# Splitting each large tile of high and low parts into two half tiles, the low ones 128 bytes on modulo 256

## The chip, the cores and the metric

The kernel runs on one core of one Trainium2 chip. Times are device microseconds (us) of one execution. The measure is the median of the runs; the profile is one further execution, recorded by the hardware profiler.

## What is computed

A gated mix of two branches over x, which has 2 batches of 4096 tokens with 640 features. Branch a is a spectral one: a real FFT over the 4096 tokens, at each frequency a two-layer complex perceptron in 4 blocks of 160 features with ReLU between and soft shrinkage behind, and the inverse FFT. Branch b is a GEGLU network 640 to 1728 to 640.

```python
def _A_ref(x, w1, b1, w2, b2):
    Xf = rfft2(x, axes=(1, 2))          # the axis of length 1 and the 4096 tokens
    zr, zi = Xf.reshape(B, H, Wf, NB, BS).real, ....imag
    hr = einsum('bhwni,nio->bhwno', zr, w1[0]) - einsum(..., zi, w1[1]) + b1[0]
    hi = einsum(..., zi, w1[0]) + einsum(..., zr, w1[1]) + b1[1]
    hr, hi = hr * (hr > 0), hi * (hi > 0)
    # or_, oi_: the same with w2, b2; then sign(o) * max(abs(o) - 0.01, 0)
    return irfft2(or_ + 1j * oi_)
def _B_ref(x, w_gate, w_up, w_down):
    return (gelu(x @ w_gate) * (x @ w_up)) @ w_down
g = sigmoid((x * gate_w).sum(-1, keepdims=True))
return g * a + (1 - g) * b
```

## The kernel before

Every large product is made of three TensorE products of numbers with fewer bits: each operand is split into a high part (`high`, on ScalarE, line 276) and a low part (`low`, the difference, mostly on VectorE, line 279), and a product is high by high, plus high by low, plus low by high. In TensorE's terms the first operand of a matmul call is the stationary one, loaded into the array as weights (128 x 128), and the second is the moving one, streamed past it (256 or 320 columns). Every call loads its own weights.

The work goes through three stages, in an order that is written out by hand (the pool is told to keep it).

- *Gate and up products.* `quad` and `plain` handle 128 features of the inner 1728 and 512 tokens at a time, `mixed` a remainder. `quad` uses a Strassen-like scheme: sums and differences of blocks of x (`b11`, `t1` to `t5`, ...) and of the weights (`g1`, `s1` to `s4`, ...), so that seven products do the work of eight. `prod` (line 465 on) writes out the three products of each pair, `run` (line 470 on, the matmul in line 472) issues them: stationary w (made by `w_prep`), moving x (made by `x_prep`), 256 columns. Between them, at hooks, `slots` and `spread` place small steps of preparation, and the first stage of the Fourier transform, `a_step`.
- *Middle stage.* The second stage of the transform (`fwd2`), the two layers (`mlp1`: 128 features by 256 frequencies; `mlp2`: 128 frequencies by 320 features), the splitting of the results (`y_split`) and the first stage of the inverse transform (`inv1`). `mms` (matmul in line 295) issues these, through `mm3` where all three products of a pair are written out; `rest`, `zl_load` and the list `fin` load and store between them. Loads and stores go through SyncE's queue (SP) in the order of the calls: `ld` at once, `st` when `flush` is called. `wd_load` brings the prepared weights of the final stage from DRAM (`wdf`, `wdl`) into SBUF tiles `wx`, where they stay.
- *Final stage.* 32 iterations of `down`, each seven forms of a Winograd-like scheme (`b11`, `t2`, `t3`, `t1`, `b21`, `t4`, `b22`), 144 products of 320 columns in `run` with stationary `ho` (the inner activations, split by `h_op`) and moving `wx`; and `inv2`, the last stage of the inverse transform, with 12 products of 320 columns (s2s, v) for most iterations. `h_load`, `c_load` and `v_load` fetch the inputs of the next iteration.

SBUF tiles come from five tags of equal buffers, laid out one behind the other: `small` (18 of 2560 bytes per partition), `big` (18 of 5120), `tiny` (15 of 1024), a gap of 112 floats and `mid` (14 of 4096). A `big` tile holds high and low parts side by side, for instance `[P, 5, 2, P]`: five blocks of 128 numbers, each as high, then low. The tiles of x are in `mid` as high half and low half.

```python
def big(shape, dt=F32, name="big"):
    return pool.tile(shape, dt, name=name, tag="big", bufs=18)
...
for (lh, ll), (rh, rl) in pairs:
    ops += [(lh, rh), (lh, rl)] + ([(ll, rh)] if ll is not None else [])
...
for (wh, wl), (xh, xl) in zip(ws, x):
    ops += [(wh, xh), (wh, xl), (wl, xh)]
...
ops += [(hh, wh), (hh, wl)] if j == 6 and a_ in HALF else [(hh, wh), (hl, wh), (hh, wl)]
```

Of the kernel before, what the change touches and what calls it, by code (L numbers as in the profile page):

```python
# [213 lines left out]
def spectral_mix_kernel(ctx: ExitStack, tc: tile.TileContext, a):  # L214
# [30 lines left out]
    def tiny(shape, dt=F32, name="tiny"):  # L245
        return pool.tile(shape, dt, name=name, tag="tiny", bufs=15)
# [66 lines left out]
    def w_prep(t, plain=False):  # L313
# [4 lines left out]
        def gate_high():  # L318
            o["r"] = RAW.pop(t)
            o["w0"] = big([P, 5, 2, P], F32R, name="w0")  # L320
            high(o["w0"][:, :, 0], o["r"][0])

        def up_high():
            o["w1"] = big([P, 5, 2, P], F32R, name="w1")
            high(o["w1"][:, :, 0], o["r"][1])

        def up_low():
            low(o["w1"][:, :, 1], o["r"][1], o["w1"][:, :, 0])
            WG[t] = o["w0"], o["w1"]
# [18 lines left out]
        def st2():  # L348
            low(o["w0"][:, :, 1], o["r"][0], o["w0"][:, :, 0])
# [3 lines left out]
        def st3():  # L353
            g, u = o["r"]
            e = o["s"][1]
            w2 = o["w2"] = big([P, 5, 2, P], F32R, name="w2")
            high(w2[:, 0:4, 0], o["s23"])
# [3 lines left out]
        def st4():  # L361
            if not plain:
                o["w1"] = big([P, 5, 2, P], F32R, name="w1")
            w1, w2 = o["w1"], o["w2"]
            high(w1[:, 0:2, 0], o["s"][0])
            high(w2[:, 4, 0], o["s"][1][:, 0])
            low(w2[:, 0:4, 1], o["s23"], w2[:, 0:4, 0])

        def st5():
            w1, w2 = o["w1"], o["w2"]  # L370
            o["w3"] = [tiny([P, 2, P], F32R, name="w3") for k in range(2)]
            if not plain:
                high(w1[:, 2:4, 0], o["r"][1][:, 2:4])
            high(w1[:, 4, 0], o["s"][1][:, 1])
            low(w1[:, 0:2, 1], o["s"][0], w1[:, 0:2, 0])
            low(w2[:, 4, 1], o["s"][1][:, 0], w2[:, 4, 0])

        def st6():
            w1 = o["w1"]
            for k in range(2):  # L380
                high(o["w3"][k][:, 0], o["s"][2][:, k])
            if not plain:
                low(w1[:, 2:4, 1], o["r"][1][:, 2:4], w1[:, 2:4, 0])
            low(w1[:, 4, 1], o["s"][1][:, 1], w1[:, 4, 0])

        def st7():
            w0, w1, w2, w3 = (o[k] for k in ("w0", "w1", "w2", "w3"))
            for k in range(2):
                low(w3[k][:, 1], o["s"][2][:, k], w3[k][:, 0])
            mat = lambda w, i: (w[:, i, 0], w[:, i, 1])  # L390
# [3 lines left out]
                     "s4": [(w3[0][:, 0], w3[0][:, 1]), (w3[1][:, 0], w3[1][:, 1])]}  # L394
# [152 lines left out]
    def plain(key, t, hook):  # L547
# [3 lines left out]
        for q, x0, x1 in ((0, "b11", "b21"), (1, "b12", "b22")):  # L551
            x = x_of(o, x0, x1, ("k4", q))
            for h, (dst, w) in enumerate(((pg, w0), (pu, w1))):
                k = 4 * q + 2 * h
                hook(k)
                run(dst[:, 256 * q:256 * q + 256], prod([(w[:, i, 0], w[:, i, 1]) for i in range(5)], x))
# [7 lines left out]
    def mixed(key):  # L564

        o, w = XO[key], WG[NPAIR]
        ws = [(w[:, k, 0], w[:, k, 1]) for k in range(5)]
# [13 lines left out]
    def f1_load(q):  # L581
        m = min(5, 17 - 5 * q)
        F1[q] = big([P, 5, 2, P], F32R, name="f1")
        nc.gpsimd.dma_start(F1[q][:, :m], a["f1"][:, 5 * q:5 * q + m])
# [23 lines left out]
    def a_step(b, n2, h):  # L608
        xs = XS.pop((b, n2, h))
        m = n2 if n2 < 16 else 32 - n2  # L610
        f = F1[m // 5][:, m % 5]
# [4 lines left out]
        for q in range(2):  # L616
            cs = slice(320 * q, 320 * q + 320)
            pa = bank()
            nc.tensor.matmul(pa[:, :320], f[:, h], xs[:, cs], start=True, stop=True)  # L619
# [16 lines left out]
    OUT1 = {"k": 256, 0: 0, 1: 512}  # L636
    LAST1 = (896, 768)

    def prep(l, pb):
# [13 lines left out]
        def wide_high(q):  # L653
            m = o["m"][q]
            if l == 1:
                w = dm[ns[q]] = big([P, 1024], F32R, name="wm")
                high(w[:, :P], m[:, :P], -1.0)
                high(w[:, 768:800], m[:, P:BS], -1.0)
                high(w[:, 800:832], m[:, BS:BS + 32])
                high(w[:, 896:960], m[:, BS:BS + 64])  # L660
                high(w[:, 256:768].rearrange("p (c h k) -> p c h k", c=2, h=2)[:, :, 0],
                     m[:, 224:].rearrange("p (c k) -> p c k", c=2))
                return
            w = dm[ns[q]] = big([P, 2, 480], F32R, name="wm")
            high(w[:, 0, BS:], m[:, BS:])
            high(w[:, 0, :BS], m[:, :BS], -1.0)

        def wide_low(q):
            w, m = dm[ns[q]], o["m"][q]
# [3 lines left out]
            if l == 1:  # L673
                minus(w[:, P:256], m[:, :P], w[:, :P])
                minus(w[:, 832:864], m[:, P:BS], w[:, 768:800])
                low(w[:, 864:896], m[:, BS:BS + 32], w[:, 800:832])
                low(w[:, 960:], m[:, BS:BS + 64], w[:, 896:960])
                x = w[:, 256:768].rearrange("p (c h k) -> p c h k", c=2, h=2)
                low(x[:, :, 1], m[:, 224:].rearrange("p (c k) -> p c k", c=2), x[:, :, 0])
                return  # L680
            low(w[:, 1, BS:], m[:, BS:], w[:, 0, BS:], nc.gpsimd)
            minus(w[:, 1, :BS], m[:, :BS], w[:, 0, :BS])
# [794 lines left out]
```

## Time and profile before

| | |
|---|---|
| Runs, median of 3 | 2547.68 us (2546.67 to 2549.09) |
| Span of the profiled execution | 2546.4 us |
| TensorE matmuls (PE) | 2535.1 us busy, 20276 instructions |
| TensorE weight loads (PEld) | 2530.4 us busy, 20276 instructions |
| VectorE (DVE) | 2055.1 us busy, 4212 instructions |
| ScalarE (ACT) | 1502.8 us busy, 3490 instructions |
| GpSimd (POOL) | 370.2 us busy, 370 instructions |
| DMA | 483.48 MB, 190 GB/s in the mean |

The span is the time from the first to the last instruction that the profiler recorded; here it lies just below the fastest of the timed runs. Times of TensorE come from pipelined matmuls whose ends are modelled: the duration of one matmul (276 to 309 ns) is longer than the distance from its start to the next one's, so the pace is read from the time that a known number of products takes. In the rows, `bank<-wx,ho` names the output and the inputs of an instruction; `L472` is the line that issued it; "x11736" is a count; in the engine's rows of a stretch the order is PE, PEld, DVE, ACT, POOL, then the granted clock of TensorE as a share, the DMA share and GB/s. In the chain in order of time each row has the start, the length, the engine, the tile, the line and the number of instructions.

### The profile page before, as it was taken

Reading aid. Unit: us, or ns where it says so; the run is one execution under the profiler, and the core shown is the slowest. Engines: PE = TensorE matmul, PEld = TensorE weight load, DVE = VectorE, ACT = ScalarE, POOL = GpSimd, SP = SyncE. Lnnn points to the kernel's source line nnn. Section 1 sums busy time; section 2 is a strip of 40 time slices with the busy share of each in tenths; the row PEclk is TensorE's granted clock in tenths of the full one; section 3 lists DMA queues with packets and bytes.
Section 4 is the critical chain, followed back from the end, with each engine's and each line's share of the span. In section 5 each row is a group of like instructions: output and inputs, shape, how many; then the busy total and the mean of one; then the engine's idle time right before and its main releaser. Section 6 shows DMA issues by size and latency. Waiting matters only on the chain.

```text
span 2546.4 us, 54296 instructions
## 1 busy us (share of the span) xinstructions
PE 2535.1 (100%) x20276; PEld 2530.4 (99%) x20276; DVE 2055.1 (81%) x4212; ACT 1502.8 (59%) x3490; POOL 370.2 (15%) x370
## 2 busy tenths in 40 slices
PE   9999999999999999999999999999999999999999
PEld 9999999999999999999999999999999999999999
DVE  7778777777777766776667788888899999999998
ACT  6555555666665655555556777778644444445443
POOL 0000000000000000000002111111133333333332
PEclk9999999999999999999999999999999999999999
DMA  6565657676767667776667455548844444344442
GB/s 232 190 215 196 212 170 234 205 236 211 219 205 249 207 213 231 224 230 214 212 222 223 129 153 150 160 137 266 291 149 138 150 156 158 120 144 156 155 136 92
DMA packets 346060, 483.48 MB, mean 190 GB/s; under 512 B 24701, under 2 KB 222717, under 8 KB 345797
## 3 DMA queue, kind: packets, MB, share of 16 engines
q1 hardware_dynamic: 331108, 438.47, 54.5%
q0 software_dynamic: 14688, 41.56, 4.5%
q8 instruction: 159, 2.61, 0.4%
q14 instruction: 105, 0.85, 0.1%
HBM read 300.29 MB, written 179.64 MB: 188 GB/s over the span
## 4 chain that ended last, share of the span: by engine, by line
PE 97%; DMA 1%; DVE 1%; issue 0%; ACT 0%; SPq 0%; DVEq 0%; ACTq 0%
PE bank L472 77%; PE bank L295 14%; PE bank L783 3%; PE bank L619 1%; DMA wx<-wdf 1%; PE bank L861 1%; PE bank L860 1%; DMA wx<-wdl 0%; PE bank L863 0%; DVE xo L279 0%; DMA wraw<-in_wgu_dram 0%; DVE xd L430 0%; DVE h L543 0%; DVE w L279 0%; DVE wl L715 0%
## 5 line engine op out<-in xcount | busy, mean ns | idle before, releaser
L472 PE MATMUL bank<-xo,w 128*128 128x256 f32 x11736 | 1362.0, 277 | 6.3 <-ACT xo L276 5.1
L472 PEld LDWEIGHTS bank<-xo,w 128*128 128x128 f32 x11736 | 1353.0, 188 | 7.5 <-ACT xo L276 5.1
L472 PE MATMUL bank<-wx,ho 128*128 128x320 f32 x4608 | 678.6, 308 | 0.1
L472 PEld LDWEIGHTS bank<-wx,ho 128*128 128x128 f32 x4608 | 674.1, 188 | 0.6 <-DMA wx<-wdf 0.3
L498 ACT ACTIVATE u<-bank 128x256 f32<-128x256 f32 x408 | 156.7, 384 | 258.0 <-PE bank L472 252.5
L279 DVE TENSOR_TENSOR ho<-hraw,ho 128x640 fp32r<-128x640 f32 (+3 forms) x384 | 276.9, 761 | 5.0 <-ACT ho L276 3.0
L276 ACT ACTIVATE ho<-hraw 128x640 fp32r<-128x640 f32 x320 | 166.3, 574 | 64.1 <-PE bank L472 46.8
L498 ACT ACTIVATE p<-bank 128x256 f32<-128x256 f32 x204 | 78.6, 385 | 149.0 <-PE bank L472 66.4
L279 DVE TENSOR_TENSOR xo<-xraw,xo 128x512 fp32r<-128x512 f32 x209 | 142.9, 684 | 25.2 <-ACT xo L276 24.7
L531 DVE TENSOR_TENSOR u<-bank,u 128x256 f32<-128x256 f32 x204 | 85.9, 421 | 90.8 <-ACT u L498 88.2
L279 DVE TENSOR_TENSOR xs<-xr,xs 64x640 fp32r<-64x640 f32 x128 | 105.0, 820 | 58.0 <-ACT xs L276 56.0
L1165 ACT ACTIVATE uu<-bank,gs 128x320 f32<-128x320 f32 x120 | 55.0, 525 | 160.0 <-PE bank L295 157.7
L295 PE MATMUL bank<-wm,h 128*128 128x320 f32 (+1 forms) x792 | 137.8, 309 | 0.0
L540 DVE TENSOR_TENSOR u<-bank,u 128x256 f32<-128x256 f32 x204 | 85.5, 419 | 62.2 <-PE bank L472 61.3
L276 ACT ACTIVATE xo<-xraw 128x512 fp32r<-128x512 f32 x209 | 131.0, 627 | 7.1 <-DMA xraw<-in_xT_dram 5.3
L621 DVE TENSOR_TENSOR as<-bank,as 64x320 f32<-64x320 f32 x256 | 113.9, 484 | 25.0 <-ACT as L620 24.0
L295 PEld LDWEIGHTS bank<-wm,h 128*128 128x128 f32 (+1 forms) x792 | 118.6, 185 | 1.2
L276 ACT ACTIVATE ho<-hs 128x640 fp32r<-128x640 f32 (+1 forms) x128 | 71.9, 576 | 77.8 <-PE bank L472 57.7
L572 POOL MEMSET h<- 64x512 f32 x16 | 8.4, 522 | 747.7 <-PE bank L619 369.4
L514 DVE TENSOR_TENSOR p<-bank,p 128x256 f32<-128x256 f32 x204 | 86.5, 424 | 36.6 <-PE bank L472 32.2
L279 DVE TENSOR_TENSOR s2s<-s,s2s 128x320 fp32r<-128x320 f32 x128 | 111.6, 929 | 0.9 <-ACT s2s L276 0.9
L620 ACT ACTIVATE as<-bank 64x320 f32<-64x320 f32 x256 | 96.8, 427 | 16.5 <-PE bank L619 14.0
(157 smaller groups left out, 3470.7 us busy)
## 6 DMA issues: line engine op xcount, KB each, us to landing
xo<-xD SPq DMA_DIRECT2D x124, 512.0 KB
xraw<-in_xT_dram SPq DMA_DIRECT2D x225, 256.0 KB
hD<-h SPq DMA_DIRECT2D x224, 256.0 KB
hraw<-hD SPq DMA_DIRECT2D x128, 320.0 KB
xD<-xo POOLq DMA_DIRECT2D x64, 512.0 KB, 4.4
sc<-scr SPq DMA_DIRECT2D x65, 320.0 KB
xr<-in_x_dram SPq DMA_DIRECT2D x64, 320.0 KB
scr<-as SPq DMA_DIRECT2D x64, 320.0 KB
```

Source lines behind the costliest of these rows:

```text
L276: nc.scalar.activation(dst, src, AF.Copy, scale=scale)
L279: eng.tensor_sub(dst, src, hi.bitcast(F32))
L295: nc.tensor.matmul(dst, l, r, start=i == 0, stop=i == len(ops) - 1)
L472: nc.tensor.matmul(dst, l, r, start=first and i == 0, stop=i == len(ops) - 1, skip_group_check=True)
L498: copy = lambda d, s_: nc.scalar.activation(d, s_, AF.Copy)
L514: nc.vector.tensor_add(p1, A, p1)
L531: nc.vector.tensor_add(u4, C, u4)
L540: nc.vector.tensor_add(u2, C, u2)
L620: nc.scalar.activation(stg[hi, cs], pa[lo, :320], AF.Copy)
L621: nc.vector.tensor_add(stg[hi, cs], pa[hi, :320], stg[hi, cs])
L783: nc.tensor.matmul(pz[:, kp * P:(kp + 1) * P], SC[b, c, kp][:, o:o + P], ft, start=True, stop=True)
L1165: nc.scalar.activation(uu[n2][:, cs], pe[:, :320], AF.Copy, scale=gs[:, b, 0, n2:n2 + 1])
```

## The change

The tag `big` goes; instead the tags `hi` and `lo` have 18 buffers of 2560 bytes each, and `pair` returns one tile of each. Five of the 15 `tiny` buffers become `tinyl`, for the low parts of small tiles. The order in SBUF is `small`, `hi`, `tiny`, a gap of 128 bytes, `lo`, `tinyl`, a gap of 320 bytes, `mid`; the total is the same. So `lo` and `tinyl` lie 128 bytes on modulo 256, and `mid` lies where it lay modulo 256. All users of `big` take a pair. With it come:

- `mm3` writes high by high, low by high, high by low, in place of high by high, high by low, low by high. `prod` and `down` keep their order.
- Low parts of the final stage's weights that lie in `mid` start 192 bytes in (`48:1008`); the tile of the form `t1` that lies in `mid` now holds its high parts, 64 bytes in (`16:976`), and `lo` holds its low parts.
- In the second layer the low part of the weights starts 192 bytes into its tile (`48:528`); in the first layer, narrow pieces and their low parts stay in one tile.
- Loads that filled one tile become two: in `f1_load`, `i1_load` (GpSimd's queue), `wd_load` and `zl_load` (SP's queue); the store in `rest` becomes two.
- In `w_prep` the four `high` and `low` calls of `w3` become two.

Cut to the core (the other steps of `w_prep`, `prep` and `mlp1` change their indices in the same way):

```diff
-    gap = []
-
-    def big(shape, dt=F32, name="big"):
-        return pool.tile(shape, dt, name=name, tag="big", bufs=18)
+    gaps = set()
+
+    def gap(tag, n):
+        if tag not in gaps:
+            gaps.add(tag)
+            nc.gpsimd.memset(pool.tile([P, n], F32, name="gap", tag=tag, bufs=1), 0.0)
+
+    def pair(shape, dt=F32, name="pair"):
+
+        h = pool.tile(shape, dt, name=name, tag="hi", bufs=18)
+        if not gaps:
+            nc.gpsimd.memset(tiny([P, 1], name="gap"), 0.0)
+        gap("gap1", 32)
+        return h, pool.tile(shape, dt, name=name, tag="lo", bufs=18)
 
     def mid(shape, dt=F32, name="mid"):
-        if not gap:
-            gap.extend([tiny([P, 1], name="gap"), pool.tile([P, 112], F32, name="gap", tag="gap", bufs=1)])
-            for t in gap:
-                nc.gpsimd.memset(t, 0.0)
+        if "gap2" not in gaps:
+            assert gaps
+            nc.gpsimd.memset(tinyl([P, 1], name="gap"), 0.0)
+            gap("gap2", 80)
         return pool.tile(shape, dt, name=name, tag="mid", bufs=14)
 
     def small(shape, dt=F32, name="small"):
         return pool.tile(shape, dt, name=name, tag="small", bufs=18)
 
     def tiny(shape, dt=F32, name="tiny"):
-        return pool.tile(shape, dt, name=name, tag="tiny", bufs=15)
+        return pool.tile(shape, dt, name=name, tag="tiny", bufs=10)
+
+    def tinyl(shape, dt=F32, name="tinyl"):
+        return pool.tile(shape, dt, name=name, tag="tinyl", bufs=5)
...
-            ops += [(lh, rh), (lh, rl)] + ([(ll, rh)] if ll is not None else [])
+            ops += [(lh, rh)] + ([(ll, rh)] if ll is not None else []) + [(lh, rl)]
...
         def gate_high():
             o["r"] = RAW.pop(t)
-            o["w0"] = big([P, 5, 2, P], F32R, name="w0")
-            high(o["w0"][:, :, 0], o["r"][0])
+            o["w0"] = pair([P, 5, P], F32R, name="w0")
+            high(o["w0"][0], o["r"][0])
...
-            o["w3"] = [tiny([P, 2, P], F32R, name="w3") for k in range(2)]
+            o["w3"] = tiny([P, 2, P], F32R, name="w3"), tinyl([P, 2, P], F32R, name="w3")
...
-            for k in range(2):
-                high(o["w3"][k][:, 0], o["s"][2][:, k])
+            high(o["w3"][0], o["s"][2])
...
-                low(w3[k][:, 1], o["s"][2][:, k], w3[k][:, 0])
-            mat = lambda w, i: (w[:, i, 0], w[:, i, 1])
+            low(w3[1], o["s"][2], w3[0])
+            mat = lambda w, i: (w[0][:, i], w[1][:, i])
...
-        F1[q] = big([P, 5, 2, P], F32R, name="f1")
-        nc.gpsimd.dma_start(F1[q][:, :m], a["f1"][:, 5 * q:5 * q + m])
+        F1[q] = pair([P, 5, P], F32R, name="f1")
+        for h in range(2):
+            nc.gpsimd.dma_start(F1[q][h][:, :m], a["f1"][:, 5 * q:5 * q + m, h])
...
-    OUT1 = {"k": 256, 0: 0, 1: 512}
-    LAST1 = (896, 768)
+    OUT1 = {"k": P, 0: 0, 1: 2 * P}
+    LAST1 = (512, 384)
...
-            w = dm[ns[q]] = big([P, 2, 480], F32R, name="wm")
-            high(w[:, 0, BS:], m[:, BS:])
-            high(w[:, 0, :BS], m[:, :BS], -1.0)
+            dm[ns[q]] = w[:, :480], wl[:, 48:528]
+            high(w[:, BS:480], m[:, BS:])
+            high(w[:, :BS], m[:, :BS], -1.0)
...
-            t = o["t"] = big([P, 2, 2, 320], F32R, name="wl")
+            th, tl = o["t"] = pair([P, 640], F32R, name="wl")
             o["b"] = small([66, 2, 320], F32R, name="bh")
             high(o["b"], o["s"])
-            high(t[:, :, 0], o["l"])
+            n = 320 if l == 2 else 256
+            o["h"], o["lo"] = (t[:, :2 * n].rearrange("p (q c) -> p q c", q=2) for t in (th, tl))
+            high(o["h"], o["l"][:, :, :n])
             for q in range(2):
-                dl[ns[q]] = t[:, q]
+                dl[ns[q]] = o["h"][:, q], o["lo"][:, q]
...
+        z = zmid(b, c, "zz")
+        fwd2(b, c, 4 * P, z)
+        F = width(b, c)
+        for h in range(2):
+            st(dr(zld[b][c], 2 * CW * h, [[4 * CW, P], [CW, 2], [1, F]]), z[h].bitcast(F32))
...
+        t = zmid(b, c, "zl1")
+        t2 = pair([66, 2, CW], F32R, name="zl2") if F == CW else zl2[chunks.index((b, c)) % 2]
+        for h in range(2):
+            if F == CW:
+                nc.gpsimd.memset(t2[h][64:66].bitcast(F32), 1.0)
+            ld(t[h].bitcast(F32), dr(d, 2 * h * P * CW, [[CW, P], [P * CW, 2], [1, F]]))
...
-                wh, wlo = w[:, 0, o:o + 320], w[:, 1, o:o + 320]
-                ops += [(h[0][:, r, fs], wh), (h[1][:, r, fs], wh), (h[0][:, r, fs], wlo)]
-            ops += [(hA[:, fs], wl[:, 0]), (hB[:, fs], wl[:66, 1])]
+                wh, wl = w[:, o:o + 320], wlo[:, o:o + 320]
+                ops += [(h[0][:, r, fs], wh), (h[1][:, r, fs], wh), (h[0][:, r, fs], wl)]
+            ops += [(hA[:, fs], rh), (hB[:, fs], rl[:66])]
...
-            t = YS[b, c, pb, j] = big([P, 2, 2, 320], F32R, name="ys")
-            split(t[:, 0], t[:, 1], y.rearrange("p r n o -> p r (n o)"),
+            t = YS[b, c, pb, j] = pair([P, 2, 320], F32R, name="ys")
+            split(*t, y.rearrange("p r n o -> p r (n o)"),
...
-    HI = {"b11": 0, "t2": 2, "b21": 4, "t3": 5, "t1": 6, "t4": 8, "b22": 9}
-    LO = {"b11": 1, "t2": 3, "t3": 7, "b21": 10, "b22": 11, "t4": 12}
+    HI = {"b11": 0, "t2": 1, "b21": 4, "t3": 5, "t4": 8, "b22": 9}
+    LO = {"b11": 2, "t2": 3, "t3": 6, "t1": 7, "b21": 10, "b22": 11, "t4": 12}
...
-                    st(dr(wdf[j], 320 * HI[n], [[13 * 320, P], [1, 320]]), w[:, 0].bitcast(F32))
-                    st(dr(wdl, 320 * j, [[7 * 320, P], [1, 320]]), w[:, 1].bitcast(F32))
+                    st(dr(wdf[j], 320 * LO[n], [[13 * 320, P], [1, 320]]), w[:, 1].bitcast(F32))
+                    st(dr(wdl, 320 * j, [[7 * 320, P], [1, 320]]), w[:, 0].bitcast(F32))
...
-            t = big([P, 4, 320], F32R, name="wx")
-            go(t.rearrange("p h d -> p (h d)"), wdf[j], 13, 4 * part, 4)
-            for k, (n, h) in enumerate((("b11", 0), ("b11", 1), ("t2", 0), ("t2", 1)) if part == 0 else
-                                       (("b21", 0), ("t3", 0), ("t1", 0), ("t3", 1))):
-                put(n, h, t[:, k])
+            ts = pair([P, 2, 320], F32R, name="wx")
+            for h in range(2):
+                go(ts[h].rearrange("p h d -> p (h d)"), wdf[j], 13, 4 * part + 2 * h, 2)
+            for k, (n, h) in enumerate((("b11", 0), ("t2", 0), ("b11", 1), ("t2", 1)) if part == 0 else
+                                       (("b21", 0), ("t3", 0), ("t3", 1), ("t1", 1))):
+                put(n, h, ts[k // 2][:, k % 2])
         elif part == 2:
             if j < 6:
                 t = small([P, 2, 320], F32R, name="wx")
                 go(t.rearrange("p h d -> p (h d)"), wdf[j], 13, 8, 2)
                 put("t4", 0, t[:, 0])
                 put("b22", 0, t[:, 1])
-            x = mid([P, 3, 320], F32R, name="wx")
-            later.append(lambda: go(x.rearrange("p h d -> p (h d)"), wdf[j], 13, 10, 3))
+            x = mid([P, 1024], F32R, name="wx")[:, 48:1008]
+            later.append(lambda: go(x, wdf[j], 13, 10, 3))
+            x = x.rearrange("p (h d) -> p h d", h=3)
             for k, n in enumerate(("b21", "b22", "t4")):
                 put(n, 1, x[:, k])
         else:
-            x = mid([P, 1024], F32R, name="wx")
+            x = mid([P, 1024], F32R, name="wx")[:, 16:976]
             n = 3 if j < 6 else 1
             go(x[:, :320 * n], wdl, 7, j, n)
             for k in range(n):
-                WM.setdefault(j + k, {}).setdefault("t1", [None, None])[1] = x[:, 320 * k:320 * k + 320]
+                WM.setdefault(j + k, {}).setdefault("t1", [None, None])[0] = x[:, 320 * k:320 * k + 320]
             if j == 6:
-                go(x[:, 336:976], wdf[6], 13, 8, 2)
-                put("t4", 0, x[:, 336:656])
-                put("b22", 0, x[:, 656:976])
+                go(x[:, 320:], wdf[6], 13, 8, 2)
+                put("t4", 0, x[:, 320:640])
+                put("b22", 0, x[:, 640:])
...
-        t = big([P, 5, 2, P], F32R, name="ho")
-        uh, ul = (tiny([P, 2, P], F32R, name="ho") for k in range(2))
+        th, tl = pair([P, 5, P], F32R, name="ho")
+        uh, ul = tiny([P, 2, P], F32R, name="ho"), tinyl([P, 2, P], F32R, name="ho")
         src, six = HR[i].pop(name) if name in ("s1", "s3", "s4", "a22") else HR[i][name]
-        split(t[:, :, 0], t[:, :, 1], src, eng)
+        split(th, tl, src, eng)
...
-        I1.append(big([P, 5, 2, P], F32R, name="i1"))
-        nc.gpsimd.dma_start(I1[0], a["i1"])
+        I1.append(pair([P, 5, P], F32R, name="i1"))
+        for h in range(2):
+            nc.gpsimd.dma_start(I1[0][h], a["i1"][:, :, h])
```

More of the change, by code (lines that the diff above doesn't have):

```diff
@@ L555, in plain @@
                 hook(k)
-                run(dst[:, 256 * q:256 * q + 256], prod([(w[:, i, 0], w[:, i, 1]) for i in range(5)], x))
+                run(dst[:, 256 * q:256 * q + 256], prod([(w[0][:, i], w[1][:, i]) for i in range(5)], x))
                 if k < 6:
@@ L566, in mixed @@
         o, w = XO[key], WG[NPAIR]
-        ws = [(w[:, k, 0], w[:, k, 1]) for k in range(5)]
+        ws = [(w[0][:, k], w[1][:, k]) for k in range(5)]
         pm = bank()
@@ L618, in a_step @@
             pa = bank()
-            nc.tensor.matmul(pa[:, :320], f[:, h], xs[:, cs], start=True, stop=True)
+            nc.tensor.matmul(pa[:, :320], f, xs[:, cs], start=True, stop=True)
             nc.scalar.activation(stg[hi, cs], pa[lo, :320], AF.Copy)
@@ L727, in spectral_mix_kernel, with zmid @@
     chunks = [(0, 1), (0, 0)] + [(b, c) for b in range(2) for c in range(NCH) if (b, c) > (0, 1)]
-    def zmid(b, c, shape, dt=F32, name="z"):
-        return (big if wide(b, c) else mid)(shape, dt, name=name)
+    def zmid(b, c, name):
+        if wide(b, c):
+            return pair([P, 2, CW], F32R, name=name)
+        t = mid([P, 2, 2, CH], F32R, name=name)
+        return t[:, 0], t[:, 1]
     def two(b, c, name):
@@ L862, in last @@
                                  skip_group_check=True)
[L863 removed]
+            nc.tensor.matmul(dst, rk, t1, start=False, stop=True, skip_group_check=True)
         h = two(b, c, "h")
@@ L1140, in h_op @@
             low(ul, six, uh, eng)
-        HO[i, name] = [(t[:, j, 0], t[:, j, 1]) for j in range(5)] + [(uh[:, j], ul[:, j]) for j in range(2)]
+        HO[i, name] = [(th[:, j], tl[:, j]) for j in range(5)] + [(uh[:, j], ul[:, j]) for j in range(2)]
     def inv2(i):
```

124 lines of the change are left out of this document (56 added, 68 removed).

## The prediction

> **What bounds the kernel now.** I read the page first: the busy table and the slices, then the chain, then the groups.
>
> ```profile
> span 2546.4 us, 54296 instructions
> PE 2535.1 (100%) x20276; PEld 2530.4 (99%) x20276; DVE 2055.1 (81%) x4212; ACT 1502.8 (59%) x3490; POOL 370.2 (15%) x370
> PEclk9999999999999999999999999999999999999999
> ...
> PE 97%; DMA 1%; DVE 1%; issue 0%; ACT 0%; SPq 0%; DVEq 0%; ACTq 0%
> PE bank L472 77%; PE bank L295 14%; PE bank L783 3%; PE bank L619 1%; DMA wx<-wdf 1%; PE bank L861 1%; PE bank L860 1%; DMA wx<-wdl 0%; PE bank L863 0%; DVE xo L279 0%; DMA wraw<-in_wgu_dram 0%; DVE xd L430 0%; DVE h L543 0%; DVE w L279 0%; DVE wl L715 0%
> ```
>
> TensorE is busy for 2535.1 of 2546.4 us, so at most 11.3 us are waits for other engines. Its clock is granted in full in every slice. The chain is TensorE for 97%, and 77% of the span is one line, the `run` helper. Every matmul has a weight load of its own (20276 of each), both rows are full, so each weight load runs beside the matmul before it. With no idle time to remove, only the pace of the matmuls can move the end. The chain in order of time gives that pace: start, length, line, count.
>
> ```profile
> 66.91 22.38 PE bank L472 x190
> 92.94 21.54 PE bank L472 x190
> ...
> 1879.54 1.76 PE bank L295 x12
> 1881.30 21.02 PE bank L472 x144
> 1904.08 21.02 PE bank L472 x144
> ```
>
> The first two rows are the same 190 gate/up products at two paces, 117.8 and 113.4 ns, with nothing waited for inside either. So a stretch can settle into a slow or a fast pace. The last rows are the final stage: 144 products of 320 columns at 146.0 ns each, and twelve of `inv2`, an iteration of 22.78 us, 32 times. The view of one line gives duration as least/median/most:
>
> ```profile
> engine op xcount: duration ns min/median/max, first and last start us, forms
> L472 PE MATMUL bank<-xo,w x11736: 276/276/583, 5.1 to 1386.3; 128*128 128x256 f32 x199
> L472 PE MATMUL bank<-wx,ho x4608: 302/309/414, 1812.1 to 2541.6; 128*128 128x320 f32 x192
> L295 PE MATMUL bank<-wm,h x792: 304/308/315, 1393.8 to 1806.0; 128*128 128x320 f32 x192, 128*2 128x320 f32 x6
> L295 PE MATMUL bank<-s2s,v x408: 303/308/312, 1806.4 to 2520.6; 128*128 128x320 f32 x136
> L295 PE MATMUL bank<-ys,i x392: 305/309/412, 1407.3 to 1812.0; 128*128 128x320 f32 x196
> L295 PE MATMUL bank<-z,wm x384: 277/280/294, 1387.7 to 1798.7; 128*128 128x256 f32 x180, 128*128 128x258 f32 x12
> ```
>
> In the gate/up stage the median is the least value, 276: half the products or more run unhindered. In the final stage the median stands 7 ns over the least, and the 320-column products of the middle stage 4 to 5 over theirs. Something holds these up by a few nanoseconds each, and only there.
>
> **The change part by part.** *Addresses.* I call an address modulo 256, counted from the start of `big`, its residue. Now `small`, `big` and `tiny` have residue 0 (buffer sizes 2560, 5120 and 1024 are multiples of 256) and `mid` 192 (the gap of 112 floats). What I compare is the moving operand of a product with the stationary operand loaded beside it, that of the next product; their difference is the distance.
>
> Gate/up stage: x in `mid`, weights in `big`, the distance is always 192, and the pace can be 113.4. Final stage: per form the products are (hh,wh), (hl,wh), (hh,wl); stationary parts all at 0, wh at 0, wl at 0 in three of seven forms and at 192 in four. So 17 of 21 products have distance 0, and the pace is 146.0. `inv1` (ys,i) is at 0 throughout. I read this as: distance 0 costs, and 192 need not.
>
> After the change hi lies at 0, lo at 128, `mid` still at 192 (128 + 320 = 448). In the final stage, product 1 moves wh (0) while hl (128) is loaded, product 2 moves wh (0) while hh (0) is loaded, product 3 moves wl (128) while hh (0) is loaded: distances 128, 0, 128. `inv1` gets the same through the new order in `mm3`. Distance 0 falls from 17 in 21 to 1 in 3.
>
> *The price of distance 0.* The page gives the mean of the final stage's product:
>
> ```profile
> L472 PE MATMUL bank<-wx,ho 128*128 128x320 f32 x4608 | 678.6, 308 | 0.1
> L472 PE MATMUL bank<-xo,w 128*128 128x256 f32 x11736 | 1362.0, 277 | 6.3 <-ACT xo L276 5.1
> ```
>
> 308 less the least, 302, is 6 ns; over 17/21 of the products that is 7.4 ns for each at distance 0. No row shows distance 128. From below it costs what the unhindered ones cost (saving up to 6 ns per product, 4608 x 6 = 28 us); from above it costs like 0 (saving nothing). I take it as free, since it is the farthest from 0 on a ring of 256: 1/3 x 7.4 = 2.5 ns remain of 6, a saving of 3.5 x 4608 = 16 us. For `inv1`, 309 - 302 = 7 falls to 2.5: 392 x 4.5 = 1.8 us. A loss from above can't be ruled out by a row either, but 309 is the slow pace already.
>
> [...]
>
> *Will DVE let it be faster?* Final iterations by engine (busy us and counts of PE, PEld, DVE, ACT, POOL):
>
> ```profile
> 1881.30:1904.08 22.78, 22.78 (x158) 22.78 (x158) 22.27 (x38) 11.01 (x24) 8.06 (x7) 1.00 0.48 155
> 1926.86:1949.64 22.78, 22.78 (x158) 22.78 (x158) 21.45 (x39) 11.13 (x24) 8.32 (x7) 1.00 0.46 150
> ```
>
> A saving of 3.5 x 144 = 0.5 us brings an iteration to 22.28, just what DVE needs in the worse row (22.27). DVE is the next bound: beyond 16 us it takes most of any further gain, at the better row (21.45) 1.33 x 32 = 43 us at the very most.
>
> *Gate/up.* Weight order is wh, wh, wl against x at 192: distances 192, 64, 192. None becomes 0. I take no change; the bound is the slow pace, below.
>
> *`mlp2`* (wm,h): stationary at 192, moving parts at 0 and 128 now, 0, 128, 64 and 192 after. Distances are 64, 192 and 128 today, and yet the median is 4 over the least. This row speaks against my reading. I take 0, bounds 792 x 4 = 3 us either way. `inv2` (s2s,v) keeps distance 192 and only changes order; `mlp1` (z,wm) 384 x 3 = 1 us either way.
>
> *Extra instructions.* `wd_load` issues two DMAs for one in 14 cases, `zl_load` and `rest` one more each for 16 chunks, `f1_load` and `i1_load` five more on Pool; merging the `w3` copies removes a few.
>
> ```profile
> L1048 SPq DMA_DIRECT2D wx<-wdf x28: 319/428/1212, 1721.8 to 1821.5; - x28
>   DMA wx<-wdf: 0.3, 1
> L584 POOL DMA_DIRECT2D f<-in_f_dram x4 | 2.2, 547 | 0.0
> ```
>
> SP's 46 extra issues at 0.43 us are 20 us, spread over the middle stage (about 1388 to 1821 us by the rows) and beside TensorE; Pool's five are 2.7 us on an engine 15% busy. Where the cover is thin is the start of the final stage: TensorE waited 0.3 us for wx there. Queued on SP behind the doubled loads are the later wx and hraw loads; five more issues ahead of them are 5 x 0.43 = 2.1 us, the bound of a wait. I take 0.
>
> *Buffers.* `tiny` goes from 15 to 10, with 5 in `tinyl`: per final iteration 20 tiles in 15 buffers become 13 in 10 and 7 in 5. Behind a later release wait SP's hraw loads and Pool's v load, and then Pool's subtractions, with Pool busy for 8 of 22.78 us. I take 0.
>
> The sum: 2546.4 - 16.1 - 1.8 = 2528.5 us by the profiled execution. The runs have a median 1.3 us over that execution, so 2530.
>
> **The rivals.** *The gate/up stage loses its fast pace (slower).* A third of its products get distance 64, which no row of 256 columns shows, and the two paces of the same 190 products show how little it takes. At the slow pace each costs 117.8 - 113.4 = 4.4 ns more: 11736 x 4.4 = 52 us, of which I estimate 46 as some stretches are slow already. With the 18 us gained, +28: 2576. It decides the sign from 18 us / 4.4 ns = 4100 products on, 35% of the stage. For it: the 64 and 192 of `mlp2` aren't free at 320 columns. Against it: the fast pace holds over hundreds of products and returns after interruptions, and no distance becomes 0. Chance 0.36.
>
> *Only the third product pays.* Then 3912 x 4.4 = 17 us eat the 18: no change, 2547.
>
> *Addresses don't matter.* The excess could come from 320 columns alone; then no pace moves and the time is 2548. The page SBUF — State Buffer (the Trainium skill, section Who interferes with whom) gives TensorE two independent read ports, one for the moving operand and one for the weights, and says that "PE and ACT never wait on anyone"; by that rule the change does nothing. The two paces and the 309 against 302 show matmuls held up while nothing that the profile names is waited for, which speaks against it here. With the last case, chance 0.10.
>
> *Late buffers or loads* in the final stage cost more than is gained: 32 iterations x 0.8 us = 26 us, 2556. DVE's margin of 0.5 to 1.3 us speaks for it, Pool's idle time against. It decides from 0.56 us per iteration. Chance 0.04.
>
> **How the numbers follow.** The forecast and what is better than it have 0.50: 2530, with a range of its own from 2508 (28 us, the whole excess, and 10 us from slow gate/up stretches that end) to 2542. Faster 0.50, the same 0.10, slower 0.40. The range of all cases goes from 2508 to 2584, the slow gate/up stage with half of the gain; about 1 in 10 is left out on each side. A change of 0.2%, 5 us, is what a measurement can tell here.
>
> **What would show it.** Right: iterations of the final stage near 22.3 us; the median of wx,ho near 305; DVE over 98% busy there; gate/up stretches of 190 still at 21.5 us with median 276. Wrong in the price: wx,ho still at 308 or more. Wrong by the first rival: the median of xo,w at 280 or more, stretches of 190 at 22 us or more. Wrong by late loads: idle time of PE above 11.3 us, ended by DMA wx or DVE ho.

## The result, and the profile after

The kernel after takes 2575.35 us (median of 4 runs, 2574.50 to 2576.83) against 2547.69 us; the ratio is 1.011, with a 95% interval of 1.0096 to 1.0125. It is slower by 1.1%, where 2530 us had been forecast. First the page of the kernel after, whose matmul line is now L483 and whose split lines are L289 (high) and L292 (low):

```profile
span 2572.7 us, 54415 instructions
PE 2554.5 (99%) x20276; PEld 2536.1 (99%) x20276; DVE 2086.1 (81%) x4203; ACT 1492.2 (58%) x3481; POOL 364.3 (14%) x378
PEclk9999999999999999999999999999999999999999
...
PE 89%; DVE 7%; issue 3%; ACT 1%; DMA 0%; POOL 0%; SPq 0%; ACTq 0%; DVEq 0%; POOLq 0%
...
L292 DVE TENSOR_TENSOR ho<-hraw,ho 128x640 fp32r<-128x640 f32 (+3 forms) x384 | 301.7, 826 | 5.0 <-ACT ho L289 3.0
```

The chain was TensorE for 97%; now VectorE has 7% of it, and "issue" 3%. The clock is granted in full as before. The view of the matmul line says in which stage the 26.3 us of span went (duration least/median/most, then first and last start):

```profile
L483 PE MATMUL bank<-xo,w x11736: 275/276/583, 5.2 to 1386.4; 128*128 128x256 f32 x199
L483 PE MATMUL bank<-wx,ho x4608: 304/309/419, 1812.9 to 2567.8; 128*128 128x320 f32 x192
```

The gate/up stage ends at 1386.4 us (before: 1386.3), and the final stage begins at 1812.9 us (1812.1). All but 0.8 us is lost in the final stage: 754.9 us from the first of its products to the last, where it was 729.5. The chain in order of time shows one iteration there (start, length, what):

```profile
2026.31 1.29 PE bank L308 x7
2027.60 9.43 PE bank L483 x63
2037.03 0.02 issue
2037.06 0.43 ACT ho L289
2037.48 5.82 DVE ho L292 x2
...
2046.12 0.16 ACT ho L289
...
2046.45 0.83 ACT s2s L289 x2
2047.28 0.41 DVE ho L292
2047.69 0.36 DVE s2s L292
2048.05 1.35 issue
2049.40 1.02 DVE s2s L292
2050.43 0.04 issue
2050.47 1.30 PE bank L308 x7
2051.77 9.43 PE bank L483 x63
```

From L308 to L308 that is 24.16 us, where an iteration of the kernel before takes 22.78. The chain leaves TensorE after 63 products, for a VectorE split of `ho` of 5.8 us (two instructions), and comes back with `inv2` (L308), which waited for the split of `s2s`. The same stretch in the timeline of GpSimd, then of VectorE, first before and then after (start, length, last column the idle time before and what ended it; VectorE's neighbours of one line are added up):

```profile
2047.06 0.57 POOL L976 DMA_DIRECT2D v<-in_v_dram  x1 [9.90 <-PE bank L472]
2047.65 2.70 POOL L1109 TENSOR_TENSOR hraw<-hraw 128x640 f32<-128x640 f32 x2
2050.31 1.63 POOL L1116 TENSOR_TENSOR hs<-hraw 128x640 f32<-128x640 f32 x1
2053.36 0.74 POOL L1116 TENSOR_TENSOR hs<-hraw 128x256 f32<-128x256 f32 x1 [1.43 <-ACT ho L276]
```

```profile
2047.35 3.14 DVE L279 TENSOR_TENSOR ho<-hraw,ho 128x640 fp32r<-128x640 f32 x3
...
2050.93 2.20 DVE L279 TENSOR_TENSOR ho<-hraw,ho 128x640 fp32r<-128x640 f32 x3
```

```profile
2037.33 0.58 POOL L994 DMA_DIRECT2D v<-in_v_dram  x1 [11.43 <-issue]
2037.93 2.27 POOL L1129 TENSOR_TENSOR hraw<-hraw 128x640 f32<-128x640 f32 x2
2040.15 2.25 POOL L1136 TENSOR_TENSOR hs<-hraw 128x640 f32<-128x640 f32 x2
```

```profile
2035.47 1.33 DVE L292 TENSOR_TENSOR ho<-hraw,ho 128x640 fp32r<-128x640 f32 x3
2037.06 0.49 DVE L1217 TENSOR_TENSOR e<-bank,e 128x320 f32<-128x320 f32 x1 [0.26 <-PE bank L483]
2037.47 6.15 DVE L292 TENSOR_TENSOR ho<-hraw,ho 128x640 fp32r<-128x640 f32 x3
```

In both kernels GpSimd's v load stands in front of its four subtractions (`h_s3`, `h_s2`). Before, it waited for a TensorE product (L472, which reads nothing of `tiny` but `ho`), so its buffer had held a part of an earlier `ho`. After, `tiny` has 10 buffers, and the one that the v load gets held the `hraw` piece that VectorE's split of `a12` has just left (2035.47 to 2036.8): GpSimd's queue waits for a VectorE semaphore until 2036.84, and in nearly every iteration this wait ends 0.04 us behind that split. So the v load comes after the split, 9.9 us into the iteration where it was 6.5 us, the four subtractions run as one block from 2037.93 to 2042.4, and the split of `a22` that began at 2037.47 goes on past their end: three instructions that take 1.33 us undisturbed take 6.15. Before, the subtractions met the splits of both `a12` and `a22`, with a pause of 1.43 us before the last of them, and these splits took 3.14 and 2.20 us. Over these two splits VectorE loses 2.7 us before and 4.8 after.

Two numbers come from the starts of the matmuls in the trace, first to last product of the final stage (4991 distances): the gaps (distances over 160 ns, less 146 each) and the pace (the mean of the rest). Before: 0.7 us of gaps, 146.03 ns. After: 20.2 us, 147.24 ns. 19.5 us of gaps and 4872 x 1.21 ns = 5.9 us of pace make the 25.4 us.

### The profile page after: what moved, and what is told of

Same layout as the page of the kernel before. It is cut to its first block, busy times and chain, and to the rows that moved or that the text cites. A ratio compares the mean times of both kernels' runs of the same rounds, so it can differ in the third digit from the quotient of the medians.

```text
span 2572.7 us, 54415 instructions
## 1 busy us (share of the span) xinstructions
PE 2554.5 (99%) x20276; PEld 2536.1 (99%) x20276; DVE 2086.1 (81%) x4203; ACT 1492.2 (58%) x3481; POOL 364.3 (14%) x378
## 4 chain that ended last, share of the span: by engine, by line
PE 89%; DVE 7%; issue 3%; ACT 1%; DMA 0%; POOL 0%; SPq 0%; ACTq 0%; DVEq 0%; POOLq 0%
PE bank L483 69%; PE bank L308 14%; DVE ho L292 4%; PE bank L803 3%; PE bank L631 1%; DVE s2s L292 1%; ACT s2s L289 1%; PE bank L878 1%; PE bank L879 1%; DVE uu L1222 1%; ACT ho L289 0%; PE bank L881 0%; DMA zl<-zl 0%; DMA xraw<-in_xT_dram 0%; DVE xo L292 0%
## 5 line engine op out<-in xcount | busy, mean ns | idle before, releaser
L483 PE MATMUL bank<-xo,w 128*128 128x256 f32 x11736 | 1361.0, 277 | 7.4 <-ACT xo L289 5.2
L483 PEld LDWEIGHTS bank<-xo,w 128*128 128x128 f32 x11736 | 1351.8, 188 | 8.9 <-ACT xo L289 5.2
L483 PE MATMUL bank<-wx,ho 128*128 128x320 f32 x4608 | 688.9, 310 | 0.1
L483 PEld LDWEIGHTS bank<-wx,ho 128*128 128x128 f32 x4608 | 679.9, 188 | 5.1 <-DVE ho L292 2.9
L292 DVE TENSOR_TENSOR ho<-hraw,ho 128x640 fp32r<-128x640 f32 (+3 forms) x384 | 301.7, 826 | 5.0 <-ACT ho L289 3.0
L289 ACT ACTIVATE ho<-hraw 128x640 fp32r<-128x640 f32 x320 | 169.4, 572 | 154.3 <-PE bank L483 59.9
L292 DVE TENSOR_TENSOR xo<-xraw,xo 128x512 fp32r<-128x512 f32 x209 | 142.8, 684 | 25.0 <-ACT xo L289 24.4
L292 DVE TENSOR_TENSOR xs<-xr,xs 64x640 fp32r<-64x640 f32 x128 | 105.0, 820 | 57.7 <-ACT xs L289 55.2
L289 ACT ACTIVATE ho<-hs 128x640 fp32r<-128x640 f32 (+1 forms) x128 | 69.5, 567 | 135.1 <-issue 112.6
L308 PE MATMUL bank<-wm,h 128*128 128x320 f32 (+1 forms) x792 | 137.3, 308 | 0.0
L289 ACT ACTIVATE xo<-xraw 128x512 fp32r<-128x512 f32 x209 | 131.1, 627 | 6.4 <-DMA xraw<-in_xT_dram 4.6
L308 PEld LDWEIGHTS bank<-wm,h 128*128 128x128 f32 (+1 forms) x792 | 118.3, 185 | 1.2
L292 DVE TENSOR_TENSOR s2s<-s,s2s 128x320 fp32r<-128x320 f32 x128 | 111.9, 931 | 0.5 <-ACT s2s L289 0.5
L468 POOL DMA_DIRECT2D xD<-xo x64 | 34.3, 536 | 479.3 <-DVE xo L292 388.6
```

What stands on the lines that cost most here:

```text
L289: nc.scalar.activation(dst, src, AF.Copy, scale=scale)
L292: eng.tensor_sub(dst, src, hi.bitcast(F32))
L308: nc.tensor.matmul(dst, l, r, start=i == 0, stop=i == len(ops) - 1)
L468: nc.gpsimd.dma_start(xD[key[1]][:, kept], XM.pop((key, name)).rearrange("p h n -> p (h n)").bitcast(F32))
L483: nc.tensor.matmul(dst, l, r, start=first and i == 0, stop=i == len(ops) - 1, skip_group_check=True)
```

## The experiments

All ratios are against the kernel before on the same chip; gaps and pace are read as above.

| kernel | median us | ratio (95% interval) | gaps us | pace ns |
|---|---|---|---|---|
| e1_tiny_split_only | 2560.06 | 1.0048 (1.0033 to 1.0063) | 13.1 | 146.13 |
| e2_low_at_0 | 2560.71 | 1.0051 (1.0034 to 1.0068) | 12.2 | 146.60 |
| e4_low_at_192 | 2612.09 | 1.0256 (1.0240 to 1.0271) | 14.1 | 146.67 |
| e5_v_behind | 2555.11 | 1.0029 (1.0018 to 1.0040) | 0.0 | 147.40 |
| e6_before_v_behind | 2547.06 | 0.9999 (0.9989 to 1.0008) | 0.0 | 146.03 |
| e7_low_at_0_v_behind | 2551.73 | 1.0012 (1.0002 to 1.0022) | 1.1 | 146.62 |
| e8_tiny_split_v_behind | 2548.31 | 0.9999 (0.9990 to 1.0008) | 0.7 | 146.03 |
| d64_ho_at_64 | 2554.34 | 1.0027 (1.0017 to 1.0037) | 0.7 | 147.04 |
| d192_ho_at_192 | 2552.75 | 1.0019 (1.0010 to 1.0029) | 1.2 | 146.93 |
| d128_ho_at_128 | 2546.91 | 0.9996 (0.9986 to 1.0005) | 0.5 | 145.76 |
| m0_x_at_0 | 2622.50 | 1.0296 (1.0278 to 1.0315) | 0.0 | 146.58 |
| m128_x_at_128 | 2607.31 | 1.0236 (1.0219 to 1.0252) | 0.0 | 146.71 |
| m64_x_at_64 | 2593.91 | 1.0180 (1.0163 to 1.0196) | 1.1 | 145.85 |

### One part of the change alone: the small buffers

```diff
     def tiny(shape, dt=F32, name="tiny"):
-        return pool.tile(shape, dt, name=name, tag="tiny", bufs=15)
+        return pool.tile(shape, dt, name=name, tag="tiny", bufs=10)
+    def tinyl(shape, dt=F32, name="tiny"):
+        return pool.tile(shape, dt, name=name, tag="tinyl", bufs=5)
...
-        uh, ul = (tiny([P, 2, P], F32R, name="ho") for k in range(2))
+        uh, ul = (t([P, 2, P], F32R, name="ho") for t in (tiny, tinyl))
```

> The kernel before, with one part of the change alone: the 15 tiny buffers become 10 and 5 (the low parts of ho, w3 and the small constants in the 5); big tiles stay whole, no address modulo 256 moves. Theory A (fewer tiny buffers: the v load in front of GpSimd's subtractions gets a buffer that VectorE's splitting of a12 has only just left, the four subtractions run late and in one piece, one VectorE split waits for all of them, TensorE waits for VectorE): PE gaps of about 20 us in the final stage, its pace unchanged at 146.0 ns a product, 2547.7 + 20 = 2568 us. Rival B (half tiles: the splits now write whole rows in place of strided ones and lose to GpSimd for that reason, or the shifted addresses do it): no gaps, 2548 us.

Measured: +12.5 us, 13.1 us of gaps, pace as before. The v load takes over the `hraw` piece of `a12` here too. So the buffers alone make most of the gaps, without any half tile or moved address, and rival B falls. The size was off: 13 us, not 20.

### The kernel after without the shift, and with another

```diff
-        gap("gap1", 32)
+        gap("gap1", 64)     # low parts at 0; 48: at 192
...
-            gap("gap2", 80)
+            gap("gap2", 48)     # 64
```

> The kernel after, gap1 256 bytes and gap2 192: the low half tiles lie at 0 modulo 256 instead of 128; all else as after. Theory A: gaps of about 20 us stay. For the pace of 147.2 ns: if the shift by 128 is what costs 1.2 ns a product, it returns to 146.0 and the time is 2575 - 6 = 2569 us; if the lost change of the moving operand from 0 to 192 is what costs, the pace is about 146.8, and the time 2573 us. Rival B' (the shift causes the stalls of VectorE too): 2548 us.

Measured: 2560.71 us, less than either case. The pace is 146.60 ns, near the second case, but the gaps shrink to 12.2 us, about those of the small buffers alone. So the shift by 128 bytes costs 0.64 ns a product (3 us) and 8 us of gaps; the other 2 us lie ahead of the final stage. In the trace about half of the iterations with the shift take some 24.2 us, most of these with a split of 5.6 us; without it they alternate between 23.0 and 23.45 us, with longest splits of 1.7 and 5.1 us. The starts in the traces tell the patterns apart. With the shift, the first instruction of the split of `a22` keeps its 0.81 us where it begins 0.50 us or more ahead of GpSimd's block, and is held to the block's end where it begins 0.48 us ahead or less. At 0 it leads by 0.49 to 0.51 us in every second iteration and is free there. That is 0.03 us earlier in the iteration, behind 63 products that take 0.64 ns less each, 0.04 us together. So the slower pace may be what tips it; no run changes that lead alone, and it stays open.

> The kernel after, gap1 192 bytes and gap2 256: the low half tiles lie at 192 modulo 256. Theory A: gaps of about 20 us stay. Pace: in the kernel before a product whose moving operand lies at 0 takes 143.4 ns when the next one's lies at 192, else 146 to 147; one in three is of this kind here, so (146.8 + 143.4 + 146.1) / 3 = 145.4 ns, 2575 - 1.8 x 4872 = 2566 us. If no address matters: 147.2 ns and 2575 us. In the gate/up stage stationary low parts at 192 meet x at 192; if that distance of 0 costs as in the final stage, a third of 11736 products lose 4.4 ns: +17 us.

Measured: 64.6 us slower, in a stage that wasn't the suspect. The gate/up stage:

```profile
L483 PE MATMUL bank<-xo,w x11736: 276/281/582, 5.1 to 1432.6; 128*128 128x256 f32 x199
L483 PE MATMUL bank<-wx,ho x4608: 303/308/417, 1859.3 to 2605.4; 128*128 128x320 f32 x192
```

The median goes from 276 to 281, and the final stage begins 47 us late. I had allowed for a third of the products, 17 us, but the whole stage runs at the slow pace, 117.8 ns in each of the chain's stretches of 190. That distance 0 is what does it isn't shown: with x at 64 (below) the same pace comes with no product at distance 0. The final stage didn't gain: 146.67 ns, not 145.4.

### The v load behind the subtractions

```diff
                     if k == 2 and n > 1:
                         c_load(n)
-                        v_load(n)
                     if k == 4:
                         h_s3(n, nc.gpsimd)
                         h_s2(n, nc.gpsimd)
+                        if n > 1:
+                            v_load(n)
```

> The kernel after, with the v load issued by GpSimd behind the subtractions h_s3 and h_s2 (at hook 4) instead of at hook 2; addresses, buffers and half tiles as after. Theory A: nothing late stands in front of the subtractions any more, the VectorE split of 5.6 us is back near 1.7 us, gaps fall from 20 us to a few, 2575 - 17 = 2558 us (the pace of 147.2 ns stays, which is 6 us). Rival B (half tiles or addresses): 2575 us.

Measured: 2555.11 us, all gaps gone. First its page, then its chain:

```profile
span 2553.3 us, 54409 instructions
PE 2541.3 (100%) x20276; PEld 2536.6 (99%) x20276; DVE 2057.8 (81%) x4203; ACT 1487.7 (58%) x3481; POOL 377.3 (15%) x378
```

```profile
1903.12 1.77 PE bank L308 x12
1904.89 21.23 PE bank L483 x144
1926.11 1.76 PE bank L308 x12
```

The chain runs through TensorE again, 144 products at 21.23 / 144 = 147.4 ns. One moved DMA issue gives back 20.2 of the 27.7 us with the layout and the number of buffers as in the kernel after (v, allocated later, may get another buffer than it did); the rest is nearly all pace.

> The kernel before, with the v load behind h_s3 and h_s2 as in the experiment on the kernel after. It has 15 tiny buffers and no PE gaps in the final stage to give back: 2548 us by theory A. If moving the load alone makes a kernel faster, whatever the buffers, it is below 2545 us and the 20 us regained after say nothing on the buffers.

Measured: no difference. Moving the load gains nothing where nothing waits for it, so what it regained in the kernel after was the wait.

> The kernel before with the tiny buffers split into 10 and 5, and the v load behind h_s3 and h_s2. If the 12.5 us of the split came by the v load's wait alone: no gaps, pace 146.0 to 146.1 ns, 2547 us. If fewer tiny buffers delay something else too: gaps of some us remain, 2550 to 2560 us.

This kernel joins the edits of e1 and e5. Measured: no difference from before, pace 146.03 ns. So all 12.5 us of the small buffers hang on the place of the v load.

> The kernel after with both suspects taken away: low half tiles at 0 modulo 256, and the v load behind h_s3 and h_s2. If the two are the whole loss but for the pace of this layout (146.6 ns in the run with low parts at 0): no gaps, 4991 x 0.57 = 2.8 us over the kernel before, 2550 us. If half tiles or their doubled loads cost something by themselves: 2553 us or more, or gaps.

The kernel after with the edits of e2 and e5. Measured: 2551.73 us, 0.12% over the kernel before, with 1.1 us of gaps and a pace of 146.62 ns: 4991 x 0.59 = 2.9 us. Beyond this pace, whose cause is open, half tiles, doubled loads and the new order in `mm3` cost nothing that these runs can tell.

### The distance in the final stage

These three kernels are the one before, with TensorE reading `ho` at other addresses:

```diff
-        HO[i, name] = [(t[:, j, 0], t[:, j, 1]) for j in range(5)] + [(uh[:, j], ul[:, j]) for j in range(2)]
+        f, fh = t.rearrange("p j h n -> p (j h n)"), uh.rearrange("p j n -> p (j n)")
+        cut = lambda x, k, last: x[:, P * k + (-48 if k == last else 16):][:, :P]    # 128: -32, 32; 192: -16, 48
+        HO[i, name] = [(cut(f, 2 * j, 9), cut(f, 2 * j + 1, 9)) for j in range(5)] + [(cut(fh, j, 1), ul[:, j]) for j in range(2)]
```

> The kernel before; in the final stage TensorE reads its stationary operand ho 64 bytes on modulo 256 (16 floats on, the last block 48 floats back; the low parts of the two small blocks stay), so the products are of the wrong numbers there; every instruction, load and wait is the same. Theory D (the prediction's: distance 0 between moving operand and the next stationary one costs 7 ns a product, another distance none): with the moving operand at 0 the distance is 192, as in the gate/up stage, and the pace goes from 146.0 towards 140 ns; VectorE's 21.5 to 22.3 us an iteration hold it at about 22.2 us: 2547.7 - 32 x 0.6 = 2528 us. Theory N (the distance does not set the pace of 320 columns): 2548 us.

> The same with ho 192 bytes on modulo 256 (48 floats on, the last block 16 back): distance 64, and 0 where the moving low parts lie at 192. Theory D: 17 of 21 products gain up to 7 ns, 2530 us. Theory N: 2548 us.

> The same with ho 128 bytes on modulo 256: distance 128 in nearly every product, with no buffer and no wait changed. The prediction took distance 128 as free: then as at 64, 2528 us. If distance 128 costs what the kernel after shows (147.2 to 147.4 ns): 5000 x 1.3 = 6 to 7 us more, 2554 us. Theory N: 2548 us.

Measured: no distance gains anything that can be told. At 64 and 192 the stage is 5 us longer, clear of the noise; at 128 it is 1.5 us shorter, within it. The products of one iteration in the chain of each (64, then 192, then 128):

```profile
1885.58 21.18 PE bank L472 x144
```

```profile
1903.93 21.16 PE bank L472 x144
```

```profile
1904.73 20.98 PE bank L472 x144
```

147.1, 146.9 and 145.7 ns. The products of 320 columns don't come near 140 ns in the mean at any distance, and theory D falls. Distance 128 is not dear in itself either, so the 147.2 to 147.4 ns of the kernel after aren't simply its price. What makes them, some 1.2 ns a product, is open: no rule in the residues was found that gives the pace of all these layouts.

### The distance in the gate/up stage

```diff
-            gap.extend([tiny([P, 1], name="gap"), pool.tile([P, 112], F32, name="gap", tag="gap", bufs=1)])
+            gap.extend([tiny([P, 1], name="gap"), pool.tile([P, 64], F32, name="gap", tag="gap", bufs=1)])   # 96: 128, 80: 64
```

> The kernel before with a gap of 256 bytes instead of 448, so that mid (x in the gate/up stage, some low parts of wx in the final stage) lies at 0 modulo 256 like everything else. In the run with low parts at 192, where a third of the gate/up products had distance 0 to x, the whole stage went from 113.8 to 117.7 ns a product and the final stage began 47 us later. If distance 0 is what does it, the same here: final stage 47 us later, 2547 + 47 = 2594 us, plus up to 4 us in the final stage where the low parts now lie at 0 too. If only that layout did it (low parts at 192, weights at two residues): 2548 us.

> The same with a gap of 384 bytes, mid at 128 modulo 256: distance 128 in every gate/up product. If 128 is as free as 192 and 64 are in that stage: 113.8 ns, 2548 us, give or take 5 us of the final stage, whose pace has been between 145.8 and 147.4 ns in all layouts so far. If 128 costs as 0 does: 2594 us.

> The same with a gap of 320 bytes, mid at 64 modulo 256: distance 64 in every gate/up product, where the kernel after had it in a third of them at no cost: 113.8 ns, 2548 us, give or take 5 us of the final stage. The prediction's first rival (distance 64 throws the stage into the slow pace): 2594 us.

Measured: all three much slower, nearly all of it by the gate/up stage. The same 190 products in the chain, which take 21.54 us in the kernel before (its row at 92.94), with x at 0, then 128, then 64:

```profile
96.65 22.80 PE bank L472 x190
```

```profile
95.11 22.55 PE bank L472 x190
```

```profile
94.44 22.38 PE bank L472 x190
```

120.0, 118.7 and 117.8 ns, in every such stretch, where the kernel before has 113.4 in all but its first; the final stage begins at 1884.2, 1866.6 and 1858.5 us instead of 1812.1. I expected this of 0 only. The rival by which addresses don't matter falls with these runs. Of the four places only 192 lets the stage run fast. The place isn't all of it: at 192 the kernel before has 117.8 ns in its first stretch, and the kernel after has distance 64 in a third of these products and loses nothing.

### 256 columns in the final stage

```diff
-                wh, wl = WM[j][b_]
+                wh, wl = (x[:, :256] for x in WM[j][b_])
```

with `acc`, `e`, `c1` and `c2` cut to 256 columns.

> The kernel before with 256 of the 320 columns in the products of down and in what VectorE and ScalarE do with them (64 columns of branch b are left out on each side, so the output is incomplete); addresses as before. If the 6 ns over the floor in the final stage are the price of distance 0, the products take 117.7 ns between waits; if they belong to the 320 columns, 113.4 ns as in the gate/up stage. VectorE, 20 us an iteration, now sets the time: about 32 x 2.5 us less than before, 2470 us, and gaps.

Measured: 2505.44 us, ratio 0.9836 (0.9820 to 0.9851). The products:

```profile
L472 PE MATMUL bank<-wx,ho 128*128 128x256 f32 x4608 | 561.5, 282 | 22.5 <-DVE ho L279 21.7
```

The mean is 282 ns where the gate/up stage has 277; from the starts, products with moving and next stationary operand at 0 follow one another at 118.9 ns, close to the 120.0 ns of the run with x at 0. So at 256 columns the final stage too has the slow pace, 5 to 6 ns over the fast one of the gate/up stage; it is at 320 columns that leaving distance 0 gains nothing. Whether at 256 columns another place would bring this stage to 113.4 ns, no run tests. The time was misjudged: an iteration stays at 21.4 us, since VectorE sets it (busy for 197.25 of the 200 us from 1900 on).

## Why the prediction was wrong

**Buffers: "I take 0".** This step failed, and with it the sign. The prediction named the queue (Pool's v load, then Pool's subtractions) and how few buffers there would be, and waved the wait away because Pool is busy for only 8 of 22.78 us. Idle time isn't the point: GpSimd's subtractions lengthen VectorE's. The same four subtractions, 3.4 us later and in one block, make one instruction of a split 5.6 us long instead of 0.8, on an engine with 0.5 to 1.3 us to spare. The term measured 20.2 us (e5 against after), of which the small buffers alone make 12.5 (e1, e8); the rest comes with the shift (e2). The prediction's own sign of it came: TensorE idle for 2572.7 - 2554.5 = 18.2 us, above 11.3.

**The price of distance 0: a gain of 16 + 2 us.** It failed too. The final stage lost 5.9 us of pace instead, and `inv1` gained nothing (median of ys,i 310 after, 309 before). The step read a mean 6 ns over the least value as the price of the one thing that looked different from the gate/up stage, and the stages differ in more, 320 columns against 256 among it. At 320 columns the final stage stayed at 145.8 to 147.0 ns with `ho` at 64, 128 or 192 (d64, d128, d192), and at 146.6 with every product at distance 0 (m0), so distance 0 has no such price there. What its 146 ns are made of stays open. The row of `mlp2`, which the prediction itself called contrary, was the better witness.

**The gate/up stage: no change.** Right, 1386.4 against 1386.3 us. The first rival's 2576 us is the measured time to within 1 us, but by coincidence: none of it is in that stage. Its mechanism is real (with x at 64 throughout, the stage loses 46 us), only not with a third of the products.

**VectorE as the next bound.** Right: its margin decides what a stall costs. **Extra instructions: 0.** Right within the 0.8 us by which the final stage begins later, and e7 bounds all of it together at some 3 us. The fourth rival, late buffers at 0.8 us an iteration for 26 us, was the right mechanism with nearly the right loss; it had been given a chance of 0.04 and was set against gains that didn't come.

## What to carry to other kernels

When a ring of buffers is cut, follow each tile that is allocated from it to the tile it takes over and that one's last reader, and see what stands behind the new wait on its queue; an engine's idle share doesn't tell whether it may be late. Where GpSimd and VectorE subtract side by side, count GpSimd's work against VectorE's margin, and ask which instruction it will meet. A pace that differs between two stages has as many suspects as the stages have differences: change one of them alone before it is given a price.

## What the runs showed of the hardware

- The pace of matmuls depends on where their operands lie: with stationary operands at 0 modulo 256 bytes, stretches of 190 products of 256 columns took 113.4 ns a product with the moving one at 192 (117.8 in the first stretch), 117.8 at 64, 118.7 at 128 and 120.0 at 0. That addresses repeat at 256 bytes is how they were counted; no run tests it. At 320 columns the pace was 145.7 to 147.4 ns in all layouts tried. The page SBUF — State Buffer (the Trainium skill, section Who interferes with whom) gives TensorE an independent read port for each operand and has it wait on no one. The trace has up to 6.6 ns a product that hang on addresses, and no run shows what the products wait for.
- A VectorE subtraction can be held up to the end of a whole row of GpSimd's. The longest of a kind (least/median/most ns, before and after):

```profile
L279 DVE TENSOR_TENSOR ho<-hraw,ho x384: 276/812/3271, 1807.2 to 2531.6; 128x640 fp32r<-128x640 f32 x128, 64x128 fp32r<-64x128 f32 x32, 128x128 fp32r<-128x128 f32 x32
```

```profile
L292 DVE TENSOR_TENSOR ho<-hraw,ho x384: 276/419/5642, 1808.0 to 2557.7; 128x640 fp32r<-128x640 f32 x128, 64x128 fp32r<-64x128 f32 x32, 128x128 fp32r<-128x128 f32 x32
```

  In the kernel after, the first instruction of the split of `a22` (128x640) kept its 0.81 us in eight iterations, where it began 0.50 us or more ahead of four subtractions in a row. With a lead of 0.46 to 0.48 us it took 5.6 us, thirteen times; begun behind the start of the first, 4.6 to 5.1 us, seven times. The lead isn't the whole rule: in the kernel before, with a lead of 0.30 us, such an instruction took 0.81 us in some iterations and 3.27 in others.

  The same page and section says that a VectorE instruction with two inputs in SBUF contends with a GpSimd instruction that reads SBUF; the trace agrees. The page also says (section SBUF: two separate sides) that the one that starts first holds the ports for its whole length. In the records the held split of 2037.47 starts 0.47 us before GpSimd's first subtraction, though 0.13 us behind the v load's issue, and still ends after the last of four, 5.6 us for 0.8; taken by recorded starts, that part isn't borne out here.
